# A fused state-space and channel-mixing kernel: its outer products in 64x32 tiles, more of them sharing a visit with other small-tile work

## The chip, the cores and the metric

The kernel runs on one core of one Trainium2 chip. The time is the device time of one execution in microseconds; several executions give a median. A profile is one execution taken by the hardware profiler. TensorE, which is PE in the rows, does the matrix products, and its weight loads are listed apart as PEld; VectorE is DVE, ScalarE is ACT, GpSimd is POOL and SyncE is SP. The last two mostly issue DMAs here.

## What is computed

The input x is 2048 tokens of 576 channels. After a layer norm it goes two ways: through a long convolution along the tokens, whose kernel K comes from 128 complex exponentials for each channel, and through a two-layer MLP for each token. The ways meet in a product.

```python
xn = layernorm(x)                                   # 2048 x 576
dt = exp(log_dt); A = -exp(log_A_real) + 1j * A_imag
C  = (C_real + 1j * C_imag) * dt[:, None]           # 576 x 128
P  = exp((A * dt[:, None])[:, :, None] * arange(2048))
K  = 2.0 * einsum("dn,dnl->dl", C, P).real
s  = irfft(rfft(xn, 4096) * rfft(K, 4096), 4096)[:2048] + xn * D_skip
h  = gelu(layernorm(xn) @ w1 + b1)                  # 4608 hidden
g  = silu(h @ w2 + b2)
out = x + s * g
```

All of it is in fp32. The MLP's matrices are split into a high and a low part in fp32r, and three products of parts stand for one.

## The kernel before

TensorE's work is of two kinds. The first is the MLP. The 4608 hidden columns come in 12 groups of three pieces of 128, the tokens in two halves of two blocks of 512, which makes 48 slots. A slot has layer 1 (`layer1`, its matmuls at L617, 128x512) for three pieces and then layer 2 (`layer2`, L680, 128x288) in eight steps. Between them `hidden` puts each piece through the GELU on ScalarE, a rounded copy on ScalarE (L656) and the low part on VectorE (L659).

The second kind is the convolution, in small tiles of the TensorE array, run on visits between steps of the MLP. The channels come in six chunks of 96 (`chunk`). Each chunk has

- stage 1 of the tokens (`x1`, matmuls at L1099 in tiles of 64 rows by 128 columns) and of the convolution kernel (`k1`, L1130, 32x128), both fed by a high and a low part made in `in_parts` (L1075 and L1079) and followed by transposes on VectorE (L1107, L1138);
- stage 2 (`s2`, L1160, 64x32, four times a chunk), followed by a copy on ScalarE (L1169) and complex products and sums on VectorE (L1175, L1181, L1182);
- the inverse (`inverse`, L1202, 32x64, two times a chunk) and the last stage (`i1`, L1228, 128x64), whose results go to memory.

The convolution's kernel is itself made on the chip in 36 batches of 16 channels. For each batch `load_par` (L896) loads parameters by a DMA that POOL issues, `tables` makes phases, sines and magnitudes on VectorE and ScalarE and weighs them (`weigh`, L950 to L956), and `kgen` forms the outer products (L995): for each channel, a product over the 128 exponentials, on the 128 rows of the array, of a table U of 32 columns and a table v of 64, real and imaginary part accumulated. Four channels stand side by side in the four column tiles of 32, so that a batch has 32 matmuls of fp32 in 128x32 tiles. The tables U and v lie in tiles of their own beside w, which holds the sines.

The order of all instructions is written out when the program is built. `Order` keeps a clock for each engine and a list of lines of steps, each with an engine, a reckoned duration, marks that it needs and a mark that it sets. After each step of the MLP, `pe_turns` decides whether small-tile work is put there. Outer products go alone, at the earliest `ALONE` after they could if the next batch's tables are not yet made or their due time isn't reached; or they ride: `ride` hands them to the stage that is put there (`GUEST`, `lead`), which then records them inside its own visit, in PSUM columns 384 to 511 of the host's bank. The inverse takes no riders. The clock then adds KG for the rider. At a slot's edge `pair` (L600) does the remaining 64 rows of layer 1 for two pieces side by side, in 64x128 tiles, in place of two full matmuls.

The durations that the planner reckons with are these:

```python
X1, S2, INV, I1, KG = 1.5, 1.75, 2.15, 3.05, 1.03
ALONE, DUE = 12.0, (160.0, 950.0)
```

In the first 50 us the rows of the input are loaded. `rest_of_norms` issues the loads of the last eight rows of tokens, and the step that issues them is reckoned to take 6 us until they land; behind it stand the statistics of those rows on VectorE (L407).

Of the kernel before, what the change touches and what calls it, by code (L numbers as in the profile page):

```python
# [18 lines left out]
P = 128  # L19
# [20 lines left out]
def dve(n):  # L40
    return 0.075 + 0.00104 * n
# [169 lines left out]
def mixer_kernel(ctx, tc, u, log_a_real, a_imag, c_real, c_imag, log_dt, d_skip, w1, b1, w2, b2,  # L211
# [38 lines left out]
    idp = sb.tile([P, P], F32, name="idp")  # L250
# [112 lines left out]

    def table_memory():

        t = [sb.tile([P, 2, SB, NV], F32, name="w", bufs=2) for _ in range(2)]
        t = [x.rearrange("p k c t -> p (k c t)") for x in t + [sb.tile([P, 2, SB, 64], F32, name="v")]]
        return [t[k // 3][:, k % 3 * D:(k % 3 + 1) * D] for k in range(8)]
# [418 lines left out]
    def params():  # L787
# [8 lines left out]
        dt = sb.tile([P, 2, SB, 32], F32, name="U").rearrange("p a b c -> p (a b c)")[:, :D]  # L796
# [94 lines left out]
    def load_par(b):  # L891
        if b == NB:
            return
        PAR[b] = sb.tile([P, SB, NPAR], F32, name="par", bufs=2)

        nc.gpsimd.dma_start(PAR[b].rearrange("p (g i) k -> p g (i k)", g=4), dram(  # L896
            par_s, (b // 3 * 48 + b % 3 * 4) * NPAR, [[D * NPAR, P], [12 * NPAR, 4], [1, 4 * NPAR]]))
# [7 lines left out]
    def tables(b):  # L905
# [5 lines left out]
        def phase(k):  # L911
            if k == 0:
                T["w"] = sb.tile([P, 2, SB, NV], F32, name="w", bufs=2)
# [28 lines left out]
        def weigh(k, part):  # L942

            if k == 0 and part == 0:
                T["v"] = sb.tile([P, 2, SB, 64], F32, name="v")
                T["U"] = sb.tile([P, 2, SB, 32], F32, name="U")
                TAB[b] = (T["U"], T["v"])
            w, v, m = T["w"], T["v"], T["m"]
            if part == 0:
                nc.vector.tensor_mul(T["U"][:, k], w[:, k, :, 33:], m[:, :, 64:])  # L950
            elif part == 1:
                nc.vector.tensor_mul(v[:, k, :, :32], w[:, k, :, 32:0:-1], m[:, :, :32])
            elif k == 0:
                nc.vector.tensor_mul(v[:, k, :, 32:], w[:, k, :, :32], m[:, :, 32:64])
            else:
                nc.vector.scalar_tensor_tensor(v[:, k, :, 32:], w[:, k, :, :32], -1.0, m[:, :, 32:64],  # L956
# [6 lines left out]
                 step("DVE", dve(SB * NV), f(phase, 0), need=[("wu", b - 2, 1)] if b > 1 else []),  # L963
# [6 lines left out]
                + [step("DVE", dve(n), f(weigh, k, part), need=[("sin", b, k)] + ([("kg", b - 1)] if b else []),  # L970
                        mark=("wu", b, k) if part == 2 else None) for k in range(2) for part in range(3)])
# [763 lines left out]
```

## Time and profile before

| | |
|---|---|
| median of 3 runs | 1099.31 us (1099.19 to 1099.48) |
| the profiled execution, as timed | 1101.59 us |
| its span from first to last instruction | 1099.8 us |
| granted clock of TensorE | 0.999 |
| HBM read and written | 102.17 MB and 36.63 MB |

A row of a group reads: source line, engine, operation, tile written, arrow, tiles read, for matmuls the array tile as rows*columns, shape and count; then busy time in us and the mean ns of one; then the idle time of the engine just before them and what ended it. A row of the timeline reads: start in us, from first start to last end in us, engine, line, operation and count. Matmuls overlap, so the time that a block takes is seen from its first start to the first start of what follows. "mxa" and "mxb" are the MLP's PSUM banks, "cv" those of the convolution.

### The profile page before, as it was taken

What the parts mean: (1) busy time and instruction counts of PE and PEld (TensorE: products, weight loads), DVE (VectorE), ACT (ScalarE), POOL (GpSimd) and SP (SyncE); (2) the same over time, 40 slices, a digit from 0 to 9 for tenths busy, and PEclk for the clock granted to TensorE, in tenths of its full rate; (3) what the DMA queues carried; (4) which work ended last, traced back from release to release, by engine and by line L of the source; (5) the groups of instructions that cost most, each with busy time, mean ns of one, the idle gap of its engine ahead of it and who ended that gap; (6) DMA issues with size and microseconds to landing.
All of it is one profiled execution on the core that took longest, in us unless ns stands there. A gap on an engine that the chain in (4) does not pass through costs nothing.

```text
span 1099.8 us, 27208 instructions
## 1 busy us (share of the span) xinstructions
PE 1089.1 (99%) x11445; PEld 953.2 (87%) x11445; DVE 918.8 (84%) x1514; ACT 698.0 (63%) x1044; POOL 184.0 (17%) x255
## 2 busy tenths in 40 slices
PE   8999999999999999999999999999999999999997
PEld 7889989889888888888898888888888888888897
DVE  7698678979998899999999998898998986766356
ACT  6485699867667675676865857566775754324233
POOL 4557211161110100001100000000100012110220
PEclk9999999999999999999999999999999999999999
DMA  8836656735434252355623315242333426453453
GB/s 222 242 131 169 219 173 197 215 71 130 152 115 152 53 112 57 100 128 149 154 51 95 96 56 126 39 143 59 94 89 78 145 66 178 117 178 107 128 148 94
DMA packets 139651, 138.23 MB, mean 126 GB/s; under 512 B 88952, under 2 KB 105016, under 8 KB 138952
## 3 DMA queue, kind: packets, MB, share of 16 engines
q1 hardware_dynamic: 124664, 85.49, 29.6%
q0 software_dynamic: 14384, 50.27, 14.8%
q8 instruction: 89, 1.46, 0.6%
q10 hardware_dynamic: 480, 0.74, 0.3%
q14 instruction: 34, 0.28, 0.1%
HBM read 102.17 MB, written 36.63 MB: 126 GB/s over the span
## 4 chain that ended last, share of the span: by engine, by line
PE 95%; DMA 2%; SPq 2%; DVE 1%; issue 0%; ACTq 0%; ACT 0%; DVEq 0%
PE mxb L680 21%; PE mxa L680 21%; PE mxa L617 20%; PE mxb L617 20%; PE cv L995 3%; PE cv L1160 3%; PE cv L1202 2%; PE cv L1228 2%; PE cv L1130 1%; PE cv L1099 1%; SPq L808 1%; DMA w<-in_A_u_dram 1%; DMA acc<-in_A_u_dram 0%; DVE st L407 0%; DMA h<-in_B_b_dram 0%
## 5 line engine op out<-in xcount | busy, mean ns | idle before, releaser
L659 DVE TENSOR_TENSOR hl<-h,hh 128x512 fp32r<-128x512 f32 x144 | 98.8, 689 | 89.0 <-ACT hh L656 88.3
L680 PE MATMUL mxb<-w2h,hl 128*128 128x288 f32 x576 | 170.2, 295 | 1.8 <-DVE hl L659 1.8
L680 PE MATMUL mxb<-w2h,hh 128*128 128x288 f32 x576 | 171.6, 298 | 0.0
L680 PE MATMUL mxa<-w2h,hh 128*128 128x288 f32 x573 | 170.8, 298 | 0.0
L680 PE MATMUL mxb<-w2l,hh 128*128 128x288 f32 x576 | 169.5, 294 | 0.0
L680 PE MATMUL mxa<-w2h,hl 128*128 128x288 f32 x573 | 169.2, 295 | 0.0
L680 PE MATMUL mxa<-w2l,hh 128*128 128x288 f32 x573 | 168.6, 294 | 0.0
L653 ACT ACTIVATE h<-mxa,b1t 128x512 f32<-128x512 f32 x73 | 50.2, 689 | 110.9 <-PE mxa L617 109.9
L680 PEld LDWEIGHTS mxa<-w2h,hh 128*128 128x128 f32 x573 | 107.6, 188 | 6.6 <-issue 3.5
L680 PEld LDWEIGHTS mxb<-w2h,hh 128*128 128x128 f32 x576 | 108.1, 188 | 5.7 <-issue 1.8
L680 PEld LDWEIGHTS mxb<-w2h,hl 128*128 128x128 f32 x576 | 108.1, 188 | 2.3 <-DVE hl L659 2.3
L680 PEld LDWEIGHTS mxb<-w2l,hh 128*128 128x128 f32 x576 | 108.1, 188 | 0.6
L680 PEld LDWEIGHTS mxa<-w2l,hh 128*128 128x128 f32 x573 | 107.6, 188 | 0.7
L680 PEld LDWEIGHTS mxa<-w2h,hl 128*128 128x128 f32 x573 | 107.5, 188 | 0.1
L896 POOL DMA_DIRECT2D par<-par_s x36 | 27.8, 773 | 462.9 <-DVE mg L939 458.4
L656 ACT ACTIVATE hh<-h 128x512 fp32r<-128x512 f32 x144 | 90.6, 630 | 3.6
L653 ACT ACTIVATE h<-mxb,b1t 128x512 f32<-128x512 f32 x71 | 48.9, 689 | 68.8 <-PE mxb L617 66.4
L690 DVE TENSOR_TENSOR acc<-mxa,acc 128x576 f32<-128x576 f32 x87 | 65.5, 752 | 31.2 <-PE mxa L680 30.9
L617 PE MATMUL mxa<-XH,w1h 128*128 128x512 f32 x284 | 79.1, 400 | 0.0
L690 DVE TENSOR_TENSOR acc<-mxb,acc 128x576 f32<-128x576 f32 x88 | 66.1, 752 | 15.2 <-PE mxb L680 14.8
L617 PE MATMUL mxb<-XH,w1h 128*128 128x512 f32 x280 | 77.7, 399 | 0.0
L617 PE MATMUL mxa<-XL,w1h 128*128 128x512 f32 x284 | 76.1, 390 | 0.0
(269 smaller groups left out, 2483.8 us busy)
## 6 DMA issues: line engine op xcount, KB each, us to landing
raw<-in_B_w_dram SPq DMA_DIRECT2D x72, 288.0 KB, 3.4
raw<-in_B_w_dram SPq DMA_DIRECT2D x96, 192.0 KB, 3.8
par_s<-A POOLq DMA_DIRECT2D x4, 2160.0 KB, 8.2
par<-par_s POOLq DMA_DIRECT2D x36, 240.0 KB, 3.4
f2t<-f2q SPq DMA_DIRECT2D x24, 256.0 KB, 3.4
g2t<-g2p SPq DMA_DIRECT2D x24, 256.0 KB, 4.1
bias<-XR SPq DMA_DIRECT2D x42, 128.0 KB, 3.7
raw<-in_B_w_dram SPq DMA_DIRECT2D x48, 96.0 KB, 3.9
```

Of the source, the lines that this page charges most:

```text
L617: nc.tensor.matmul(q, a, b, start=j == 0 and i not in BEGUN, stop=j == len(ops) - 1, skip_group_check=True)
L653: nc.scalar.activation(t, q, AF.Gelu_apprx_tanh, bias=b1t[:, k:k + 1], scale=1.0)
L656: LAST[0] = nc.scalar.activation(hh[:, i], t, AF.Copy)
L659: nc.vector.tensor_sub(hl[:, i], t, hh[:, i].bitcast(F32))
L680: nc.tensor.matmul(q[:, dh, :288], a[:, i, c], b[:, i, d], start=i == 0 and k == 0 and not alone, stop=i == G - 1 and k == 2)
L690: nc.vector.tensor_add(o, q[:, dh:dh + n, :288], b)
L808: nc.sync.dma_start(r[32 * g:32 * g + 32].rearrange("c (b n) -> c b n", n=32), dram(src[k], 32 * g, [[N, 32], [32 * N, D // 32], [1, 32]]))
L896: nc.gpsimd.dma_start(PAR[b].rearrange("p (g i) k -> p g (i k)", g=4), dram(par_s, (b // 3 * 48 + b % 3 * 4) * NPAR, [[D * NPAR, P], [12 * ...
L995: nc.tensor.matmul(q[32 * g:32 * g + 32, i // 2, i % 2 * 64:i % 2 * 64 + 64], U[:, ri, 4 * g + i, :], v[:, ri, 4 * g + i, :], start=ri == ...
L1160: nc.tensor.matmul(Q[i][32 * q:32 * q + 32, f, 2 * ri:2 * ri + 2], m[r, 4 * i + q, 32 * ri:32 * ri + 32], A2[r, 4 * p + 2 * i + q // 2, :, ...
L1202: nc.tensor.matmul(QI[q // 2][64 * f:64 * f + 64, q % 2, i], MAT["g2t", p + i // 2][r, i % 2, f, ri], YS[p + i // 2][0][r, i % 2, ri, f], ...
L1228: nc.tensor.matmul(Q[h][64 * y:64 * y + 64, t], g1t.rearrange("p a e -> p (a e)"), A2[:, k:k + 2, 1].rearrange("p i d r -> p i r d"), star ...
```

## The change

**Outer products.** `load_par` now loads a batch so that the upper 64 partitions hold other channels than the lower 64, and the 128 exponentials of a channel lie in two places of the same 64 partitions; four DMAs do it in place of one. `kgen` has 64 matmuls in 64x32 tiles: for each channel four accumulate, of two halves and two parts. U and v are now views of one tile with w, which `weigh` fills in place in four instructions instead of six.

**Rides.** A batch's outer products need one mark of the weighing (`wu`), the wait for the next batch's tables is for `wu` and not for the sines, and `ALONE` is 20 instead of 12. In stage 1 of the tokens the rider is recorded behind the host's matmuls instead of ahead of them. A ride with stage 2 is reckoned 0.14 us shorter than KG.

**Around them.** Stage 1's input is first put in order by one more copy on ScalarE, so that the high and the low part read contiguous memory. Transposes behind stage 1 are half as many and twice as long. Stage 2's results lie in another order in PSUM, its copy on ScalarE also writes a negated part, and products and sums are one instruction each. The last tokens' loads are reckoned 7 us instead of 6.

```diff
@@ -247,7 +247,7 @@
-    idp = sb.tile([P, P], F32, name="idp")
+    idp = sb.tile([P, 4, P], F32, name="f2t")[:, 0]
...
@@ -361,11 +361,13 @@
+    def table_tile():
+        return sb.tile([P, 2, SB, 32 + NV], F32, name="w", bufs=2)
+
     def table_memory():
-        t = [sb.tile([P, 2, SB, NV], F32, name="w", bufs=2) for _ in range(2)]
-        t = [x.rearrange("p k c t -> p (k c t)") for x in t + [sb.tile([P, 2, SB, 64], F32, name="v")]]
-        return [t[k // 3][:, k % 3 * D:(k % 3 + 1) * D] for k in range(8)]
+        t = [table_tile().rearrange("p k c t -> p (k c t)") for _ in range(2)]
+        return [t[k // 4][:, k % 4 * D:(k % 4 + 1) * D] for k in range(8)]
...
@@ -893,8 +895,12 @@
-        nc.gpsimd.dma_start(PAR[b].rearrange("p (g i) k -> p g (i k)", g=4), dram(
-            par_s, (b // 3 * 48 + b % 3 * 4) * NPAR, [[D * NPAR, P], [12 * NPAR, 4], [1, 4 * NPAR]]))
+        for h in range(2):
+            for e in range(2):
+                nc.gpsimd.dma_start(
+                    PAR[b][64 * h:64 * h + 64, 8 * e:8 * e + 8].rearrange("p (g i) k -> p g (i k)", g=4), dram(
+                        par_s, (64 * e * D + b // 3 * 48 + b % 3 * 4 + 2 * h) * NPAR,
+                        [[D * NPAR, 64], [12 * NPAR, 4], [1, 2 * NPAR]]))
...
@@ -939,36 +946,34 @@
-        def weigh(k, part):
-
-            if k == 0 and part == 0:
-                T["v"] = sb.tile([P, 2, SB, 64], F32, name="v")
-                T["U"] = sb.tile([P, 2, SB, 32], F32, name="U")
-                TAB[b] = (T["U"], T["v"])
+        def weigh(part):
+
+            if part == 0:
+                TAB[b] = (T["w"][:, :, :, 33:], T["v"][:, :, :, :64])
             w, v, m = T["w"], T["v"], T["m"]
             if part == 0:
-                nc.vector.tensor_mul(T["U"][:, k], w[:, k, :, 33:], m[:, :, 64:])
+                nc.vector.tensor_mul(v[:, :, :, :32], w[:, :, :, 32:0:-1], bc(m[:, :, :32], 1, 2))
             elif part == 1:
-                nc.vector.tensor_mul(v[:, k, :, :32], w[:, k, :, 32:0:-1], m[:, :, :32])
-            elif k == 0:
-                nc.vector.tensor_mul(v[:, k, :, 32:], w[:, k, :, :32], m[:, :, 32:64])
+                nc.vector.tensor_mul(w[:, :, :, 33:], w[:, :, :, 33:], bc(m[:, :, 64:], 1, 2))
+            elif part == 2:
+                nc.vector.tensor_mul(w[:, 0, :, :32], w[:, 0, :, :32], m[:, :, 32:64])
             else:
-                nc.vector.scalar_tensor_tensor(v[:, k, :, 32:], w[:, k, :, :32], -1.0, m[:, :, 32:64],
+                nc.vector.scalar_tensor_tensor(w[:, 1, :, :32], w[:, 1, :, :32], -1.0, m[:, :, 32:64],
...
-                 step("DVE", dve(SB * NV), f(phase, 0), need=[("wu", b - 2, 1)] if b > 1 else []),
+                 step("DVE", dve(SB * NV), f(phase, 0), need=[("kg", b - 2)] if b > 1 else []),
...
-                + [step("DVE", dve(n), f(weigh, k, part), need=[("sin", b, k)] + ([("kg", b - 1)] if b else []),
-                        mark=("wu", b, k) if part == 2 else None) for k in range(2) for part in range(3)])
+                + [step("DVE", dve((2, 2, 1, 1)[part] * n), f(weigh, part), need=[("sin", b, 1)],
+                        mark=("wu", b) if part == 3 else None) for part in range(4)])
...
@@ -989,18 +994,21 @@
             Q.append(q)
-            for i in range(SB // 4):
-                for ri in range(2):
+            for i in range(2):
+                for k in range(4):
+                    ri, e = divmod(k, 2)
                     for g in range(4):
-                        nc.tensor.matmul(q[32 * g:32 * g + 32, i // 2, i % 2 * 64:i % 2 * 64 + 64], U[:, ri, 4 * g + i, :],
-                                         v[:, ri, 4 * g + i, :], start=ri == 0, stop=ri == 1, skip_group_check=True)
+                        for h in range(2):
+                            f, t = slice(64 * h, 64 * h + 64), 8 * e + 2 * g + i
+                            nc.tensor.matmul(q[32 * g:32 * g + 32, h, 64 * i:64 * i + 64], U[f, ri, t, :], v[f, ri, t, :],
+                                             start=k == 0, stop=k == 3, skip_group_check=True)
...
-        return [step("PE", KG + 0.2, mm, need=need + [("wu", b, 1)], cv=1, mark=("kg", b)),
+        return [step("PE", KG + 0.2, mm, need=need + [("wu", b)], cv=1, mark=("kg", b)),
...
@@ -1013,7 +1021,7 @@
         GUEST.append(st["fn"])
-        host["dur"] += KG
+        host["dur"] += KG - 0.14 * (host["mark"][0] == "s2")
...
@@ -1068,19 +1076,28 @@
+            T = {}
+
+            def turn():
+                T["x"] = sb.tile([P, 24, m], F32, name="xt")
+                nc.scalar.activation(T["x"], get(), AF.Copy)
+
+            def source():
+                return get() if which == "k" else T["x"].rearrange("p c b -> p (c b)")
+
             def high():
-                a = sb.tile([P, 2, 4 * CH], F32R, name="pr").rearrange("p t c -> p (t c)")
-                b = sb.tile([P, 2, 4 * CH], F32R, name="ys", bufs=2).rearrange("p t c -> p (t c)")
-                PARTS2[which, i] = [t.rearrange("p (c b) -> p c b", b=m) for t in (a, b)]
-                nc.scalar.activation(PARTS2[which, i][0], get(), AF.Copy)
+                T["a"] = sb.tile([P, 2, 4 * CH], F32R, name="pr").rearrange("p t c -> p (t c)")
+                T["b"] = sb.tile([P, 2, 4 * CH], F32R, name="ys", bufs=2).rearrange("p t c -> p (t c)")
+                PARTS2[which, i] = [T[k].rearrange("p (c b) -> p c b", b=m) for k in "ab"]
+                nc.scalar.activation(T["a"], source(), AF.Copy)
             def low():
-                a, b = PARTS2[which, i]
-                nc.vector.tensor_sub(b, get(), a.bitcast(F32))
-
-            n = 768 if which == "k" else 2000
-            four.append(step("ACT", act(n), high, need=need))
-            four.append(step("DVE", dve(n), low, mark=(which + "p", c, i)))
+                nc.vector.tensor_sub(T["b"], source(), T["a"].bitcast(F32))
+
+            if which == "x":
+                four.append(step("ACT", act(2000), turn, need=need))
+            four.append(step("ACT", act(768), high, need=need if which == "k" else ()))
+            four.append(step("DVE", dve(768), low, mark=(which + "p", c, i)))
...
@@ -1091,21 +1108,20 @@
                     Q[24 * v] = q[:, :, :384].rearrange("p e (d b) -> p e d b", b=32)
-                lead(q)
...
+                lead(q)
...
-                for e in range(2):
-                    c0 = 48 * i + d0 + 12 * e
-                    add("DVE", 0.65, lambda d0=d0, e=e, c0=c0: nc.vector.transpose(
-                        A2[:, :, 0, c0:c0 + 12].rearrange("p k d r -> p d k r"), Q[d0][:, e]), cv=-e)
+                c0 = 48 * i + d0
+                add("DVE", 0.9, lambda d0=d0, c0=c0: nc.vector.transpose(
+                    A2[:, :, 0, c0:c0 + 24].rearrange("p k d r -> p d k r"), Q[d0]), cv=-1)
...
@@ -1134,11 +1150,9 @@
             add("PE", X1, mm, cv=2, mark=("k1", c, i), need=[("kp", c, i)] + ([("i1", c - 1)] if c and i == 0 else []))
-            for g in range(4):
-                add("DVE", 0.65, lambda g=g: nc.vector.transpose(
-                    A2[:, :, 1, 48 * i + 12 * g:48 * i + 12 * g + 12].rearrange("p k d r -> p d k r"),
-                    Q[g // 2 * 2][:, g % 2]),
-                    cv=-(g % 2))
+            for g in (0, 2):
+                add("DVE", 0.9, lambda g=g: nc.vector.transpose(
+                    A2[:, :, 1, 48 * i + 12 * g:48 * i + 12 * g + 24].rearrange("p k d r -> p d k r"), Q[g]), cv=-1)
...
@@ -1157,7 +1171,7 @@
                                 r = slice(64 * f, 64 * f + 64)
-                                nc.tensor.matmul(Q[i][32 * q:32 * q + 32, f, 2 * ri:2 * ri + 2],
+                                nc.tensor.matmul(Q[i][32 * q:32 * q + 32, f, ri::2],
...
@@ -1165,25 +1179,26 @@
             def copy(i):
-                KK[i] = sb.tile([P, 2, 2, CH], F32, name="kk")
-                nc.scalar.activation(KK[i], Q[i][:, :, 1::2], AF.Copy)
+                KK[i] = sb.tile([P, 2, 3, CH], F32, name="kk")
+                nc.scalar.activation(KK[i][:, :, :2], Q[i][:, :, :1:-1], AF.Copy)
+                nc.scalar.activation(KK[i][:, :, 2], Q[i][:, :, 3], AF.Copy, scale=-1.0)
...
-                PR[i] = sb.tile([P, 2, 4 * CH], F32, name="pr").rearrange("p t (a b d) -> p t a b d", a=2, b=2)
-                for t in range(2):
-                    nc.vector.tensor_mul(PR[i][:, t], bc(Q[i][:, t, 0::2], 2, 2), bc(KK[i][:, t], 1, 2))
+                PR[i] = sb.tile([P, 2, 4 * CH], F32, name="pr").rearrange("p t (a c) -> p t a c", a=2)
+                x, k = Q[i].rearrange("p t k d -> p t (k d)")[:, :, :2 * CH], KK[i].rearrange("p t k d -> p t (k d)")
+                k = bass.AP(tensor=k.tensor, offset=k.offset + CH, ap=[list(k.ap[0]), list(k.ap[1]), [-CH, 2], [1, 2 * CH]])
+                nc.vector.tensor_mul(PR[i], bc(x, 2, 2), k)
...
-                nc.vector.tensor_sub(y[:, i, 0], x[:, :, 0, 0], x[:, :, 1, 1])
-                nc.vector.tensor_add(y[:, i, 1], x[:, :, 0, 1], x[:, :, 1, 0])
+                nc.vector.tensor_add(y[:, i].rearrange("p a t d -> p t a d"), x[:, :, :, :CH], x[:, :, :, CH:])
             for i in range(2):
-                two.append(step("ACT", act(4 * CH), lambda i=i: copy(i), need=[("s2", c, p)]))
-                two.append(step("DVE", 0.95, lambda i=i: prod(i), cv=-1))
-                two.append(step("DVE", 0.63, lambda i=i: sums(i), mark=("sum", c, p) if i else None))
+                two.append(step("ACT", act(4 * CH) + act(2 * CH), lambda i=i: copy(i), need=[("s2", c, p)]))
+                two.append(step("DVE", dve(8 * CH), lambda i=i: prod(i), cv=-1))
+                two.append(step("DVE", dve(4 * CH), lambda i=i: sums(i), mark=("sum", c, p) if i else None))
...
@@ -1456,7 +1471,7 @@
             x_load(b)
-    nl["steps"].append(step(None, 6.0, rest_of_norms))
+    nl["steps"].append(step(None, 7.0, rest_of_norms))
...
@@ -1518,7 +1533,7 @@
     EDGE = 0.2, 0.6
-    ALONE, DUE = 12.0, (160.0, 950.0)
+    ALONE, DUE = 20.0, (160.0, 950.0)
...
@@ -1536,7 +1551,7 @@
                     b = kl["steps"][0]["mark"][1]
-                    wait = ("sin", b + 1, 1) not in od.marks or od.t["PE"] < DUE[0] + b * (DUE[1] - DUE[0]) / NB
+                    wait = ("wu", b + 1) not in od.marks or od.t["PE"] < DUE[0] + b * (DUE[1] - DUE[0]) / NB
...
```

More of the change, by code (lines that the diff above doesn't have):

```diff
@@ L795, in params @@
         flat = lambda t: t.rearrange("p a b -> p (a b)")
[L796 removed]
+        dt = ys_tile().rearrange("p i a b c -> p (i a b c)")[:, :D]
         PRM = [flat(sb.tile([P, 12, 64], F32, name="kt", bufs=2)) for _ in range(2)]
@@ L912, in phase @@
             if k == 0:
-                T["w"] = sb.tile([P, 2, SB, NV], F32, name="w", bufs=2)
+                T["v"] = table_tile()
+                T["w"] = T["v"][:, :, :, 32:]
                 nc.vector.tensor_mul(T["w"][:, 1], bc(PAR[b][:, :, 0], 2, NV), bc(tv, 1, SB))
```

2 lines of the change are left out of this document (1 added, 1 removed).

## The prediction

> **What bounds the kernel now.** First the page: its shares of busy time, then its chain of work that ended last.
>
> ```profile
> span 1099.8 us, 27208 instructions
> PE 1089.1 (99%) x11445; PEld 953.2 (87%) x11445; DVE 918.8 (84%) x1514; ACT 698.0 (63%) x1044; POOL 184.0 (17%) x255
> PE 95%; DMA 2%; SPq 2%; DVE 1%; issue 0%; ACTq 0%; ACT 0%; DVEq 0%
> ```
>
> TensorE is busy 99% of the span and carries 95% of the chain. Next, what TensorE waited for in the whole execution:
>
> ```profile
> PE mxb L680 <- DVE hl L659: 1.8, 2, 1.2
> PE mxa L1290 <- POOL XL L1283: 1.3, 1, 1.3
> PE cv L500 <- DVE row L440: 1.1, 1, 1.1
> PE mxa L632 <- ACT XH L504: 0.4, 1, 0.4
> ```
>
> That is 4.6 us, all before 50 us. So the end is set by the sum of TensorE's own work. Work saved on VectorE or added on ScalarE moves nothing while it only fills idle time; a microsecond of TensorE moves the end by one. The third view groups TensorE's instructions by shape; these are the groups that the change bears on:
>
> ```profile
> L995 PE MATMUL cv<-v,U 128*32 128x64 f32 x2304 | 39.6, 221 | 0.0
> L1160 PE MATMUL cv<-A,f2t 64*32 64x192 f32 x1536 | 38.6, 332 | 0.0
> L1202 PE MATMUL cv<-ys,g2t 32*64 32x96 f32 x1536 | 21.9, 253 | 0.0
> ```
>
> Each fp32 matmul of the source shows as two MATMUL records and two weight loads: the outer products (L995) are 1152 in the source and 2304 here, 36 blocks of 64. Stage 2 (L1160) is 24 blocks of 64, the inverse (L1202) 12 blocks of 128. These durations overlap, so the price of a block is read from the timeline as the distance from its first start to the next block's first start:
>
> ```profile
> 361.57 0.29 PE L680 MATMUL mxb<-w2l,hh 128*128 128x288 f32 x1
> 361.70 0.29 PE L680 MATMUL mxb<-w2h,hl 128*128 128x288 f32 x1
> 361.92 1.10 PE L995 MATMUL cv<-v,U 128*32 128x64 f32 x64
> 362.95 0.40 PE L680 MATMUL mxa<-w2h,hh 128*128 128x288 f32 x1
> 363.19 0.29 PE L680 MATMUL mxa<-w2l,hh 128*128 128x288 f32 x1
> ...
> 296.54 1.58 PE L1160 MATMUL cv<-A,f2t 64*32 64x192 f32 x64
> 298.05 0.40 PE L680 MATMUL mxa<-w2h,hh 128*128 128x288 f32 x1
> ...
> 440.12 1.10 PE L995 MATMUL cv<-v,U 128*32 128x64 f32 x64
> 441.15 1.62 PE L1160 MATMUL cv<-A,f2t 64*32 64x192 f32 x64
> 442.70 1.21 PE L617 MATMUL mxb<-XH,w1h 128*128 128x512 f32 x4
> ...
> 325.66 1.83 PE L1202 MATMUL cv<-ys,g2t 32*64 32x96 f32 x128
> 327.42 1.20 PE L617 MATMUL mxb<-XH,w1h 128*128 128x512 f32 x4
> ```
>
> Outer products alone take 361.92 to 362.95, 1.03 us. Going in costs 0.22 instead of the usual 0.13 from start to start, and the first MLP matmul behind takes 0.24 instead of 0.13: 0.20 us for each visit that the small tiles pay between MLP matmuls. Stage 2 takes 1.51 alone and 1.55 behind outer products, the inverse 1.76.
>
> **The outer products in 64x32 tiles.** The same multiplications now come as 64 source matmuls a block over eight tiles (two halves of the rows, four of the columns) instead of 32 over four: 128 records and 128 weight loads instead of 64 and 64. No row shows this. By columns nothing changes: 64 records over four tiles are 16 rounds of 64 columns, 1024 in 1.03 us, 1.0 ns a column; 128 over eight are again 16 rounds of 64. Lower end: 1.03 us. Stage 2, also over eight tiles, keeps that rate: 8 rounds of 192 columns, 1536, in 1.51. But it has only 64 records. The inverse has 128 over eight tiles, 16 rounds of 96, the same 1536 columns, and takes 1.76: 0.22 to 0.25 more than its columns ask. So many short records have a price that columns do not explain. Upper end: a new block is as long as the inverse, 1.76. How the inverse loses it, in two narrow stretches of the timeline:
>
> ```profile
> 325.66 0.43 PEld L1202 LDWEIGHTS cv<-ys,g2t 32*64 32x64 f32 x33 [0.35 <-issue]
> 325.66 0.59 PE L1202 MATMUL cv<-ys,g2t 32*64 32x96 f32 x32
> ```
>
> The stretches end at 326.04. The first 32 matmuls have started after 0.35 us (0.59 less the 0.24 of the last one), 11 ns each, and only one weight load stands beyond them. The other 96 need the remaining 1.41 us, 14.7 ns each. I read this as a limit on how many instructions TensorE holds at once: after 32 pairs the next must wait until an early matmul has ended, and that wait goes by a matmul's whole duration, not by its columns. The old outer products escape it: 64 pairs at a slower beat, two batches.
>
> [...]
>
> For the new block: the first 32 at the rate of columns, 16 pairs a round-time of 112 ns, 0.22 us; the other 96 like the inverse's, 1.41 us, times the ratio of the durations in the rows above, 221/253: 1.23. Together **1.45 us**, 0.42 more than now, 36 blocks: **+15.1 us**. Other readings lie on both sides: the inverse's excess as a fixed 0.23 gives 1.26, its late beat kept whole 0.22 + 1.41 = 1.63.
>
> **Rides.** In the two programs' instruction order, runs of small-tile work between MLP matmuls are 84 before and 76 after; 18 of 36 outer products stand alone before and 10 after. Eight visits less at 0.20: **-1.6 us**. Twelve outer products share a visit with stage 2 in both. After the change both are in 64x32 tiles. What a shared shape saves is seen where the paired remainder (L600) and stage 1 (L1099), both 64x128, stand side by side:
>
> ```profile
> 254.31 0.50 PE L600 MATMUL mxb<-XR,w1s 64*128 64x512 f32 x1
> 254.65 0.51 PE L1099 MATMUL cv<-pr,f2t 64*128 64x384 f32 x4
> 255.81 0.96 PE L617 MATMUL mxb<-XH,w1h 128*128 128x512 f32 x3
> ...
> 240.36 0.62 PE L1099 MATMUL cv<-pr,f2t 64*128 64x384 f32 x4
> 241.63 1.20 PE L617 MATMUL mxa<-XH,w1h 128*128 128x512 f32 x4
> ...
> 439.69 0.50 PE L600 MATMUL mxb<-XR,w1s 64*128 64x512 f32 x1
> ```
>
> Side by side 0.34 and 1.16; alone stage 1 takes 1.27, and ahead of outer products L600 takes 0.43 (439.69 to 440.12). That saves 0.20; the lower end is the 0.04 by which stage 2 is longer behind outer products. I take 0.15, twelve times: **-1.8 us**. Moving the rider behind stage 1's matmuls puts stage 1 next to L600 in two visits, as in two before: nothing. Two more L600 pairs replace four full matmuls: under 0.1.
>
> **The last tokens' landing.** VectorE takes its work in order, and L407 waits there for the loads:
>
> ```profile
> 43.78 0.82 DVE L407 BATCH_NORM_STATS2 st<-w 128x6 f32<-128x288 f32 x2 [3.77 <-DMA w<-in_A_u_dram]
> 44.94 0.46 DVE L407 BATCH_NORM_STATS2 st<-w 128x6 f32<-128x288 f32 x1
> 45.32 0.67 DVE L659 TENSOR_TENSOR hl<-h,hh 128x512 fp32r<-128x512 f32 x1
> ```
>
> TensorE's 1.8 us on L659 is this. In the changed order only the statistics at 44.94 move behind L659; the two at 43.78, which wait for the load, stay ahead. So 0.4 comes back: **-0.4 us** (0 to -1.8).
>
> **VectorE, ScalarE, POOL.** The merged table products, transposes, products and sums save starts of instructions, and the contiguous low part saves more; stage 1's input is copied once more on ScalarE:
>
> ```profile
> L1079 DVE TENSOR_TENSOR ys<-xc,pr 128x768 fp32r<-128x768 f32 x12 | 24.7, 2056 | 1.8 <-ACT pr L1075 1.6
> L1079 DVE TENSOR_TENSOR ys<-kt,pr 128x768 fp32r<-128x768 f32 x12 | 11.1, 927 | 0.0
> L1075 ACT ACTIVATE pr<-kt 128x768 fp32r<-128x768 f32 x12 | 10.1, 838 | 4.3 <-PE cv L1099 3.8 <-ACT w2h L570 0.3 <-PE cv L1130 0.3
> L896 POOL DMA_DIRECT2D par<-par_s x36 | 27.8, 773 | 462.9 <-DVE mg L939 458.4
> ```
>
> Strided against contiguous: 2056 - 927 = 1.1 us, 12 times, 14 us off VectorE; 12 x 0.84 = 10 us onto ScalarE, and 48 negating copies of at most 0.3, 14 more. The cover is TensorE's 99%: no wait on either engine ends late after 50 us, so I take 0; without the cover ScalarE's 24 us would be the ceiling. L896 becomes four issues: 144 x 0.77 = 111 us on POOL instead of 28, 3.1 us a batch, behind which POOL's stores queue. POOL idled 463 us before these issues, and the load is asked for a batch ahead of its use (950 - 160 over 36 by the planner, 22 us); hidden.
>
> **Sum** against the profiled span: +15.1 - 1.6 - 1.8 - 0.4 = +11.3, 1111.1. The runs' median of 1099.31 lies 0.5 under the span of 1099.8, so **1110.6 us**.
>
> **Rivals.** First, TensorE keeps the rate of columns: a block stays at 1.03. For it: stage 2 over eight tiles at 1.51, no dearer than its columns. Against it: the inverse with the same count of records. Then -3.8 us, **1095.5**, faster; it decides up to a block of 1.07, where -3.8 + 36 x 0.04 leaves the 0.2% of gain. Second, the excess is small and the two sides meet: a block of 1.07 to 1.20 gives 1097 to 1101.5, at 1.14 **1099.5**, no change beyond the 0.2% (2.2 us) that a measurement of this kernel can tell. The inverse's fixed excess with half of it hidden (1.03 + 0.11) speaks for it. Third, the parameter loads come late through POOL's four issues: the table work then blocks VectorE with L659 behind it. At 2.3 us (3 x 0.77) for each of the three or four batches that start before 160 us, on top of the forecast, **1118**; POOL's 17% speaks against.
>
> **How the numbers follow.** Forecast, blocks of 1.26 to 1.63: 53%; by itself 36 x 0.23 - 3.8 = +4.5 to 36 x 0.60 - 3.8 = +17.8, 1104 to 1117. First rival 32%, second 12%, third 3%. The range reaches down to the first rival and leaves out the top of the forecast: 1094.8 to 1114.5. Faster 0.33, same 0.12, slower 0.55.
>
> **What would show it.** In the changed profile the outer products' group has 4608 records in tiles of 64x32. Right: about 1.45 us from the first of 128 records to the next block, the start beat slower after the first 32. Wrong: 1.03 with an even beat. Shared visits with stage 2 should be 0.15 shorter than their parts; TensorE's waits should stay near 4 us and before 50 us. A wait of TensorE on VectorE or ScalarE after 60 us would show that a cover is gone, and a wait of L939 on the parameter load the third rival.

## The result and the profile after

| | before | after |
|---|---|---|
| median of 5 runs | 1099.48 us | 1137.40 us (1136.98 to 1139.60) |
| span of the profiled execution | 1099.8 us | 1135.3 us |
| ratio, 95% interval | | 1.0346 (1.0330 to 1.0363) |

The change costs 38 us: the direction of the forecast, three times its size, and outside its range. The profiled execution of before was timed at 1101.59 us, 2.3 above the median, so the spans differ by 35.5 us where the medians differ by 37.9. The changed kernel's page, shares of busy time, chain by engine, and the queue that brings instructions; behind it that queue's row from the page of before:

```profile
span 1135.3 us, 31836 instructions
PE 1109.2 (98%) x13749; PEld 969.5 (85%) x13749; DVE 892.4 (79%) x1298; ACT 731.5 (64%) x1112; POOL 244.2 (22%) x363
PE 81%; DVE 5%; DMA 5%; ACT 4%; issue 3%; POOL 1%; SPq 0%; DVEq 0%; ACTq 0%; POOLq 0%
q8 instruction: 107, 1.75, 0.7%
```

```profile
q8 instruction: 89, 1.46, 0.6%
```

TensorE still looks full, 98%. But its part of the chain has fallen from 95% to 81%, and 3% stand at "issue", time in which nothing that the profile records held it. What TensorE waited for, in the changed kernel (us in total, times, longest):

```profile
PE cv L1174 <- issue: 8.8, 6, 2.4
PE mxa L619 <- ACT h L655: 2.4, 1, 2.4
PE mxb L682 <- DVE acc L692: 1.8, 1, 1.8
...
PE mxb L682 <- issue: 1.1, 2, 0.7
```

Two things are new: six waits in stage 2 (L1174, before L1160) with no releaser, and waits on ScalarE and VectorE, which the forecast had excluded after 50 us. The groups and the timeline of the changed kernel give the price of a new block:

```profile
L1003 PE MATMUL cv<-w 64*32 64x64 f32 x4608 | 53.7, 225 | 0.0
L1174 PE MATMUL cv<-A,f2t 64*32 64x192 f32 x1536 | 42.9, 338 | 8.8 <-issue 8.8
```

```profile
156.59 1.49 PE L1003 MATMUL cv<-w 64*32 64x64 f32 x128
158.00 0.74 PE L619 MATMUL mxb<-XH,w1h 128*128 128x512 f32 x2
```

1.41 us from first start to first start, where it was 1.03. Summed by line over both traces, as distances from start to start (a stop counts with what it takes beyond the ordinary beat, and the slower starts right behind it), the span's 35.5 us divide so:

| after less before | us |
|---|---|
| outer products, 36 blocks: 37.1 to 49.7 | +12.6 |
| stage 2, 24 blocks: 36.9 to 49.9, of it 9.9 in six stops | +13.0 |
| stops in the MLP: 2.7 to 14.0, of it about 8 between 97 and 171 us | +11.3 |
| the MLP without its stops (fewer visits, four matmuls fewer) | -2.1 |
| two more L602 pairs, the rest | +0.7 |

The forecast had the first and the fourth row; stage 2 it had with the other sign, the third row not at all. Nearly all of stage 2's 13 us lie in the six blocks that stop: they take 2.79 to 5.38 us from first start to the next block's first start, 22.0 together, while the other six behind outer products take 1.54 to 1.59, 9.4 together. One of those that run through, with the outer products ahead of it:

```profile
774.13 1.48 PE L1003 MATMUL cv<-w 64*32 64x64 f32 x128
775.42 1.65 PE L1174 MATMUL cv<-A,f2t 64*32 64x192 f32 x64
777.00 1.19 PE L619 MATMUL mxa<-XH,w1h 128*128 128x512 f32 x4
```

### The profile page after: what moved, and what is told of

Read it like the earlier page. It is cut to its first block, busy times and chain, and to the rows that moved or that the text cites. A ratio compares the mean times of both kernels' runs of the same rounds, so it can differ in the third digit from the quotient of the medians.

```text
span 1135.3 us, 31836 instructions
## 1 busy us (share of the span) xinstructions
PE 1109.2 (98%) x13749; PEld 969.5 (85%) x13749; DVE 892.4 (79%) x1298; ACT 731.5 (64%) x1112; POOL 244.2 (22%) x363
## 3 DMA queue, kind: packets, MB, share of 16 engines
q0 software_dynamic: 16112, 50.27, 15.1%
q8 instruction: 107, 1.75, 0.7%
## 4 chain that ended last, share of the span: by engine, by line
PE 81%; DVE 5%; DMA 5%; ACT 4%; issue 3%; POOL 1%; SPq 0%; DVEq 0%; ACTq 0%; POOLq 0%
PE mxb L682 17%; PE mxa L682 17%; PE mxa L619 17%; PE mxb L619 16%; PE cv L1003 4%; PE cv L1174 3%; DMA par_s<-A 2%; PE cv L1217 2%; PE cv L1146 1%; PE cv L1243 1%; PE cv L1115 1%; DMA kk<-in_f_dram 1%; DMA f2p<-in_f_dram 1%; DVE w2l L569 1%; DMA row<-y_s 1%
## 5 line engine op out<-in xcount | busy, mean ns | idle before, releaser
L900 POOL DMA_DIRECT2D par<-par_s x144 | 88.9, 633 | 350.8 <-DVE mg L946 268.7
L692 DVE TENSOR_TENSOR acc<-mxa,acc 128x576 f32<-128x576 f32 x87 | 65.5, 753 | 26.5 <-PE mxa L682 26.3
L692 DVE TENSOR_TENSOR acc<-mxb,acc 128x576 f32<-128x576 f32 x88 | 66.1, 752 | 22.7 <-PE mxb L682 22.4
```

The source lines that it names most:

```text
L692: nc.vector.tensor_add(o, q[:, dh:dh + n, :288], b)
L900: nc.gpsimd.dma_start(PAR[b][64 * h:64 * h + 64, 8 * e:8 * e + 8].rearrange("p (g i) k -> p g (i k)", g=4), dram(par_s, (64 * e * D + b // ...
```

## What the experiments showed

Three theories had to be told apart: the dearer blocks (foreseen), stops because TensorE's instructions do not arrive in time, and a changed early order that comes from one number of the planner. The ratios are to the kernel before.

**The outer products taken back out.** `load_par` and the matmuls of `kgen` are those of before; all else is as changed.

```diff
-            for i in range(2):
-                for k in range(4):
...
+            for i in range(SB // 4):
+                for ri in range(2):
                     for g in range(4):
+                        nc.tensor.matmul(q[32 * g:32 * g + 32, i // 2, i % 2 * 64:i % 2 * 64 + 64], U[:, ri, 4 * g + i, :],
```

> The changed kernel with the outer products and the parameter load put back (32 matmuls in 128x32 tiles, one DMA); tables, rides, stages and book-keeping stay as changed. Theory: three things make the 38 us: the longer blocks (36 x 0.35 to 0.39, 13 us), waits of TensorE for its own instructions around them (12 to 15 us), and an early order that makes it wait for VectorE and ScalarE between 100 and 170 us (6 to 8 us). Then this version loses the first two: 1108 to 1112 us, blocks of 1.03, no stop inside stage 2, and the early waits still there. Rival: the new steps on ScalarE and VectorE (copies, merged products) are what TensorE waits for: then it stays above 1125 us.

Measured 1112.54, 1.0117 (1.0097 to 1.0137), half a microsecond above the range of the theory. The blocks are back at 1.03 and of the stops in stage 2 one of 0.2 us is left; what stays is early:

```profile
PE mxa L619 <- ACT h L655: 5.7, 1, 5.7
```

So the new outer products cost 25 us in place of the 13 of their blocks, and the rest of the change costs 13 without them.

**The outer products alone**, put into the kernel before (the same edit the other way round).

> The kernel before with nothing but the new outer products and the four parameter loads they need. Theory: +13 us from blocks of about 1.41 instead of 1.03, and on top stops of 1 to 2.6 us inside some of the twelve stage 2 blocks that come right behind outer products, 5 to 12 us: 1117 to 1125 us, no new waits before 170 us. Rival one: no such stops, they come from the changed stage 2: 1112 us. Rival two: the blocks are longer only because of the tables' new place in memory (a row pitch of 97): 1099 to 1102 us.

Measured 1122.89, 1.0216 (1.0194 to 1.0238): 23 us again from this part. The blocks sum to 49.9 us (49.7 in the changed kernel) though U and v lie in tiles of their own as before, so the second rival, the tables' place in memory, is refuted. The stops are there (waits and timeline of this kernel), and its rides are those of before:

```profile
PE cv L1167 <- issue: 6.3, 6, 1.3
```

```profile
714.97 1.20 PE L617 MATMUL mxa<-XH,w1h 128*128 128x512 f32 x4 [0.74 <-issue]
```

The second fence shows one that is not in stage 2: it meets layer 1, behind a visit of outer products with stage 1 of the convolution's kernel. Stage 2 is not the cause, only the usual place.

**What makes a block long: records or columns.** Two kernels halve the one and the other. In the first, half of the accumulation is left out; in the second, half of v's columns, and a second copy on ScalarE fills the place.

```diff
-                for k in range(4):
+                for k in (0, 2):
...
-                                             start=k == 0, stop=k == 3, skip_group_check=True)
+                                             start=k == 0, stop=k == 2, skip_group_check=True)
```

> The changed kernel with only the first half of each accumulation in the outer products (the exponentials of the second half are left out): 64 records over eight tiles, still in stage 2's shape. Theory: TensorE holds some 32 pairs at a time, so two batches instead of four: blocks of 0.75 to 0.85 us instead of 1.41, and no stop inside stage 2, since 128 + 128 instructions are no more than before: 1098 to 1106 us with the early waits still there. Rival: the stops come from the shape that stage 2 shares with what stands ahead of it: they stay, 10 us, 1110 to 1116 us.

```diff
-                            nc.tensor.matmul(q[32 * g:32 * g + 32, h, 64 * i:64 * i + 64], U[f, ri, t, :], v[f, ri, t, :],
+                            nc.tensor.matmul(q[32 * g:32 * g + 32, h, 32 * i:32 * i + 32], U[f, ri, t, :], v[f, ri, t, :32],
```

> The changed kernel with outer products of 32 moving columns instead of 64 (half of the table v is left out, the other half is copied twice by two smaller copies): the records stay 128 a block, the columns are halved. Theory: the block goes by records and by a matmul's whole duration, which falls only by some 27 ns of 225: 1.30 to 1.38 us. Rival: it goes by columns (16 rounds of 32): 0.6 to 0.8 us. Stops inside stage 2 stay under the theory, they are about the count of instructions; time 1133 to 1138 us.

Timeline of the one with half the records, then of the one with half the columns:

```profile
156.06 0.86 PE L1003 MATMUL cv<-w 64*32 64x64 f32 x64
156.84 1.19 PE L619 MATMUL mxb<-XH,w1h 128*128 128x512 f32 x4
```

```profile
190.96 1.29 PE L1003 MATMUL cv<-w 64*32 64x32 f32 x128
192.18 0.40 PE L682 MATMUL mxa<-w2h,hh 128*128 128x288 f32 x1
```

Half the records: 0.78 us. Half the columns: 1.22, less than the 1.30 to 1.38 of the theory and far from the rival's 0.6 to 0.8. From 1.41 the first takes 0.63, the second 0.19. Half the records are half the columns too, so 0.44 of the 0.63 are left for the records alone: their number sets most of the price, as the forecast had it. That it is a limit on what TensorE holds is a reading that fits both, not shown by itself. The stops go the same way: with half the records the only wait left in stage 2 is one of 0.2 us on a DMA, with half the columns six stops remain.

```profile
L1174 PE MATMUL cv<-A,f2t 64*32 64x192 f32 x1536 | 39.3, 333 | 0.2 <-DMA f2t<-f2q 0.2
```

```profile
PE cv L1175 <- issue: 10.1, 6, 2.1
```

By time the first took 1106.35 us, the second 1136.16, one run each: halving the columns saved next to nothing of the 38 us. The first shows too how much is not outer products: its blocks are 10 us cheaper than before's, and it is 7 us slower all the same.

**Why TensorE stops: the supply of instructions.** The row of q8 above gives 1.75 MB in 107 packets, 16.4 KB each, and TensorE has 27498 records, 257 for each packet. One stop in the changed kernel, by its timeline, and the queues in the window 449 to 453:

```profile
449.67 0.59 PE L1003 MATMUL cv<-w 64*32 64x64 f32 x35
450.06 0.91 PE L1174 MATMUL cv<-A,f2t 64*32 64x192 f32 x29
452.25 1.21 PE L1174 MATMUL cv<-A,f2t 64*32 64x192 f32 x35 [1.28 <-issue]
```

```profile
q8 instruction: 1, 0.02, 1.5%
```

Stage 2 halts after 29 of its 64 matmuls and goes on at 452.25; the one packet of q8 there ran from 449.80 to 450.75 in the trace. A block of outer products with stage 2 behind it is 256 + 128 loads and matmuls in about 3 us; the MLP, with a load and a matmul every 0.13 or 0.23 us, needs 8 to 15 us for 128 instructions. The six stops in stage 2 come after 9640, 10662, 11173, 17558, 19088 and 23176 records; from one to the next are 1022, 511, 6385, 1530 and 4088, each within 15 of a multiple of 256. If pieces of 256 instructions are the cause, the stops must fall on their borders, and move over the work when something is put ahead. Two kernels put 64 and 128 short matmuls more into the warm-up, 128 and 256 instructions:

```diff
-    warm_up(16)
+    warm_up(8)
+    for _ in range(72):
+        nc.tensor.matmul(qb[:, 0, :64], zero[:, :P], zero[:, :64], start=True, stop=True)
```

> The changed kernel with 64 short matmuls more in the warm-up ahead of everything: 128 more instructions of TensorE (64 loads, 64 matmuls) before all others, the same order behind them. Theory (TensorE's instructions come in pieces of 256, and a stop falls on the border of two pieces): counted in TensorE's records of loads and matmuls, the six stops in stage 2 of the changed kernel come after 9640, 10662, 11173, 17558, 19088 and 23176 records, with rests of 168 falling to 136 by 256. Shifted by 128, the borders fall elsewhere in the work: all six of those stage 2 blocks (near 450, 484, 497, 743, 790 and 926 us) run through, and 2 to 6 stops come at others whose last 256 instructions took under 2 us: near 346, 358, 594, 614, 643 or 910 us, again with a rest of 136 to 170. Rival (something in those six blocks themselves stops them: their place in the order, their bank, what they read): the same six stop, with rests of about 10 to 40.

The second has 4 and 140 there.

> The changed kernel with 128 short matmuls more in the warm-up: 256 more instructions of TensorE before all others, the same order behind them. Theory: the borders of pieces fall on the same work again; if every border can stop TensorE, the same six stage 2 blocks stop, with the same rests. If only every other border can (borders that stopped lie mostly 512 or a multiple apart), most of the six run through and others, near 775 us among them, may stop. Rival (the blocks themselves): the same six, as also in the run with 128 more.

The waits of TensorE in the kernel shifted by 128, and its timeline; then the waits of the one shifted by 256:

```profile
PE cv L1174 <- issue: 6.9, 4, 2.7
...
PE cv L1146 <- issue: 2.3, 1, 2.3
```

```profile
357.72 0.88 PE L1174 MATMUL cv<-A,f2t 64*32 64x192 f32 x21
361.31 0.56 PE L1174 MATMUL cv<-A,f2t 64*32 64x192 f32 x11 [2.70 <-issue]
...
470.18 1.65 PE L1174 MATMUL cv<-A,f2t 64*32 64x192 f32 x64
```

```profile
PE cv L1174 <- issue: 9.9, 6, 2.8
```

The two kernels took 1150.83 and 1165.98 us, one run each; most of what they take more than the changed kernel is the longer warm-up itself, behind which the first matmul of layer 1 starts at 24.1 and 39.3 us instead of 13.0. Shifted by 128, all six old places run through; the block that stood at 450 is the one at 470.18, 64 matmuls without a break. Five of the six places named ahead stop instead (at 361, 377, 612, 634 and 926 us of this run, whose work lies 15 to 20 us later); the sixth, the one foreseen at 643, loses only 0.3 us. Shifted by 256, the same six stop as in the changed kernel. How many records had started at a stop is read from windows that end there; of the changed kernel, of the shift by 128 and by 256, with the counts of PE and PEld in brackets:

```profile
0.00:452.24 452.24, 442.36 (x4820) 391.00 (x4820) 358.75 (x552) 315.07 (x507) 146.93 (x203) 1.00 0.52 147
```

```profile
0.00:376.88 376.88, 365.39 (x3670) 326.40 (x3670) 283.17 (x451) 253.30 (x427) 134.84 (x184) 0.97 0.55 158
```

```profile
0.00:478.62 478.62, 469.43 (x4948) 419.82 (x4948) 357.78 (x552) 315.23 (x507) 147.39 (x203) 1.00 0.49 139
```

9640, 7340 and 9896 records leave 168, 172 and 168 by 256. All stops without a releaser in small tiles have such a rest, in these kernels and in the one with the outer products alone, from 179 falling to 136 as the run goes on. Three of the MLP's stops in the changed kernel (616, 644 and 913 us, 2.1 us together) have it too.

The packets of q8 tell which borders stop. In the changed kernel each of the eight stops without a releaser ends 1.4 to 1.6 us after the end of the q8 packet before it (452.25 against 450.75 above; 743.27 against 741.88 at the longest), and in the two shifted kernels and the one with the outer products alone it is 1.2 to 1.6. Packets and borders go one to one: border 37 of the run, at 9640 records, stops for the 37th packet, and so for every stop. A border near 775 us was passed without a stop, though its last 256 instructions took 1.3 us: its packet had ended at 773.03, and TensorE came to the border at 775.4, 2.4 us later. With the rests of the other borders estimated from those of the stops, nine of the changed kernel's borders were reached less than 1.4 us after the end of their packet, and these are the six stops in stage 2 and the three in the MLP; the next one came 1.6 us after and did not stop. So the cause is shown: in the changed kernel TensorE waited at a border when it came there less than about 1.4 us after the packet with the next piece had landed. What sets the time of a packet stays open: at the eight stops it starts between 251 records ahead of the border and, at the longest, only when TensorE stands there. That a shift by one piece brought the same six back shows that it is not a fixed every other one.

**Rides with stage 2 refused**, so that outer products and stage 2 stand apart.

```diff
-        if not kl["steps"] or kl["steps"][0]["eng"] != "PE" or host["mark"][0] == "inv":
+        if not kl["steps"] or kl["steps"][0]["eng"] != "PE" or host["mark"][0] in ("inv", "s2"):
```

> The changed kernel in which outer products do not ride with stage 2. Theory: the stops inside stage 2 (six of 0.9 to 2.6 us beyond the ordinary beat, 10 us) come from 256 + 128 instructions used up in 3 us; apart, they are gone, and some 3 us of slower stage 2 behind outer products go as well, while eight more visits cost 1.6 us and the shared shape's 1.3 us are lost: 1126 to 1130 us. Rival: the stops belong to stage 2's changed order of columns in PSUM and stay: 1139 to 1141 us.

Measured 1155.33, 1.0509 (1.0487 to 1.0531), a miss by time. Of the stops one of 0.5 us is left (first fence, waits; its rest by 256 is 139), and TensorE's last matmul starts 7 us earlier than in the changed kernel. But the order became another one: the last stage of the convolution ran at 1104 (timeline), 30 us later than in the changed kernel, and the chain ends in its stores and loads.

```profile
PE cv L1174 <- issue: 0.5, 1, 0.5
```

```profile
1104.11 2.92 PE L1243 MATMUL cv<-A,g1t 128*64 128x384 f32 x16
```

```profile
1108.22 4.51 DMA s_s<-ys
...
1140.80 4.60 DMA A<-s_s
```

After TensorE's last matmul 32 us of such work remain, 6 in the other kernels. It tells that the stops go when outer products and stage 2 stand apart, and that an edit of the planner cannot be priced by the part that it is meant for.

**One number of the planner: the last tokens' landing.** In the changed kernel it is put back from 7 to 6 us; in the kernel before, it is put from 6 to 7 with nothing else touched.

```diff
-    nl["steps"].append(step(None, 7.0, rest_of_norms))
+    nl["steps"].append(step(None, 6.0, rest_of_norms))
```

> The changed kernel with the last tokens' landing reckoned 6 us again. Theory: that number moved the second half of the norms and all that hangs on it on POOL some 20 us later; with 6 the waits of TensorE between 100 and 170 us go (8 us) and the two at 45 and 48 us come back (1.8 us): 1130 to 1133 us. Rival: the early order is another because of the changed tables and tiles, and the waits stay: 1136 to 1139 us.

Measured 1127.48, 1.0255 (1.0237 to 1.0274): 10 us less than the changed kernel and less than either expectation. The waits between 97 and 171 us are gone; those at 45 and 48 us, which were expected back, did not come; the stops in stage 2 stay (10.3 us, eight times, in its waits).

> The kernel before with nothing but the last tokens' landing reckoned 7 us. Theory: it takes back up to 1.8 us at 45 and 48 us and moves the second half of the norms on POOL later; if that alone makes the waits at 147 to 161 us, 1102 to 1108 us. Rival: in the kernel before the early order has room for it: 1097 to 1099 us, give or take the four visits more that its order has (0.8 us).

Measured 1111.81, 1.0116 (1.0099 to 1.0133): the number alone costs 12 us, more than the theory had. What it does is read in the timelines, first the kernel before, then the changed one:

```profile
81.28 2.79 POOL L450 TENSOR_SCALAR w<-w,mv,rs 128x576 f32<-128x576 f32 x1 [7.76 <-ACT h L653]
...
94.67 0.57 POOL L271 DMA_DIRECT2D turns_s<-in_f_dram  x1
...
138.42 0.55 POOL L883 DMA_DIRECT2D par_s<-A  x1 [11.53 <-ACT w2h L570]
...
148.99 5.31 ACT L874 ACTIVATE A<-A 128x144 f32<-128x144 f32 x18
...
155.61 0.69 ACT L653 ACTIVATE h<-mxa,b1t 128x512 f32<-128x512 f32 x1
```

```profile
93.34 2.28 POOL L452 TENSOR_SCALAR w<-w,mv,rs 128x576 f32<-128x576 f32 x1 [21.08 <-issue]
...
123.13 0.56 POOL L271 DMA_DIRECT2D turns_s<-in_f_dram  x1
...
144.29 0.58 POOL L885 DMA_DIRECT2D par_s<-A  x1 [2.48 <-DMA f2p<-in_f_dram]
...
156.63 5.26 ACT L876 ACTIVATE A<-A 128x144 f32<-128x144 f32 x18 [8.59 <-DMA par_s<-A]
...
163.21 0.69 ACT L655 ACTIVATE h<-mxa,b1t 128x512 f32<-128x512 f32 x1
```

In the changed order the norms of the last rows come 12 us later on POOL, and with them the constants (28 us later) and a store of parameters (6 us later). The kernel before with nothing but the 7 us has the same: its norms start at 93.72, its constants at 121.83, the store at 142.46. ScalarE then stood 8.59 us for that store's landing, and the rest of the table work (L876) and the GELU came only behind it: the GELU starts at 163.21 and TensorE waited for it, 2.4 us. On VectorE the same happened with the constants, and TensorE's 1.8 us on L692 are this:

```profile
147.83 0.23 DVE L294 TENSOR_TENSOR kk<-kk 128x64 f32<-128x64 f32 x1 [2.98 <-DMA kk<-turns_s]
148.99 0.75 DVE L692 TENSOR_TENSOR acc<-mxb,acc 128x576 f32<-128x576 f32 x1
```

In the kernel before with 7 us the wait is longer, and TensorE is slow behind it; its waits, and two windows (the first bare number after the busy times is the granted clock):

```profile
PE mxa L617 <- ACT h L653: 6.0, 1, 6.0
```

```profile
158.00:165.00 7.00, 1.00 (x5) 0.53 (x3) 3.67 (x4) 6.97 (x22) 0.00 (x0) 0.85 0.09 30
165.00:170.00 5.00, 5.00 (x13) 3.90 (x14) 2.63 (x3) 4.48 (x8) 0.00 (x0) 0.52 0.01 3
```

In the 5 us behind the wait only 13 matmuls ran, at a granted clock of 0.52; the kernel before has 40 there at 1.00. The changed kernel with the old outer products shows it again (5.7 us of waiting, then 12 matmuls in 5 us at 0.50); the changed kernel waits 2.4 us and stays at 1.00.

**What is left of the change.** Old outer products and 6 us together; then also the full reckoning for rides with stage 2 (`host["dur"] += KG`); then, from the first again, `ALONE` 12 instead of 20.

> The changed kernel with the old outer products and load, and the landing reckoned 6 us again. Theory: with the blocks, the supply stops and the early waits gone, what is left is the rides (12 visits less than before the change, 2.4 us), against small waits on VectorE and ScalarE of 1 to 4 us that the change's planning brings: 1097 to 1102 us. Rival: the changed stages and tables cost TensorE several microseconds by themselves: 1105 us or more.

> As the version with the old outer products and the landing of 6, with a ride with stage 2 reckoned at KG in full. Theory: the 6 us of small waits of TensorE on VectorE and ScalarE in that version come in part from a plan that reckons each such ride 0.14 us short of what the old tiles take, so that later work is planned for a TensorE that is further on than it is; then 1098 to 1100.5 us. Rival: they come from the new steps on ScalarE and the tables, whatever the reckoning: 1101 to 1103 us.

> As the version with the old outer products and the landing of 6, with ALONE at 12 us as before the change. Theory: rides are worth 0.20 us for each visit saved and nothing else, so two visits more cost 0.4 us and the time is 1101.5 to 1103 us. Rival: holding the outer products back for 20 us is what brings the small waits: 1098 to 1100.5 us.

| kernel | us | ratio |
|---|---|---|
| old products, landing 6 | 1102.03 | 1.0022 (1.0012 to 1.0031) |
| the same, full reckoning | 1102.13 | 1.0025 (1.0017 to 1.0034) |
| the same as the first, `ALONE` 12 | 1100.90 | 1.0010 (1.0002 to 1.0019) |

The first lies at the top of its theory's range, the second in its rival's, the third between the two. The reckoning of rides does nothing that can be measured; a longer `ALONE` costs about 1 us at most, the two intervals overlap. None of the three beats the kernel before. The first has no wait between 97 and 171 us and 72 visits in place of 84. Summed as above, its visits take some 2 us less, and short waits in the MLP, spread over the run, some 4 us more; two of them:

```profile
PE mxa L682 <- DVE acc L692: 1.0, 1, 1.0
PE mxb L682 <- DVE hl L661: 0.9, 2, 0.5
```

The parts add up: outer products alone +23.3 against the kernel before on the same chip, the landing alone +12.3, the rest +2.5, together 38.1 where the change costs 37.9. That they meet so closely is in part luck: taken out of the changed kernel, the outer products give 24.9 and the landing 9.9, and the two early waits are not the same length.

## Why the prediction was right or wrong

- **A block of outer products, 1.45 us, +15.1:** right. 1.41 where it stands alone, 1.28 ahead of stage 2; +12.6 in all. The first 32 matmuls start within 0.27 us (0.22 in the sum), the rest at a slower beat, as the working had it. By halving, more of it goes by the records than by the columns (0.44 to 0.19). The first two rivals, the rate of columns and the small excess, are refuted.
- **Shared shape with stage 2, 0.15 each:** right in size where nothing stops: 1.41 less 1.28 is 0.13, and stage 2 behind it is 0.02 longer than alone. But the sum took no account of what those visits bring close together, 384 loads and matmuls within 3 us. This term had the wrong sign: -1.8 forecast, some +11 with the stops.
- **Eight visits fewer, -1.6:** right as far as it can be read: the MLP without its stops is 2.1 us shorter, and 0.9 of that are four matmuls fewer at 0.23, which the two more pairs give back.
- **The missing term: the supply of instructions.** The block was priced by what TensorE does with an instruction, not by how it gets one. The page of before had a row on it, q8 with 89 packets for 22890 records, and from that the 107 could be reckoned, but not the waiting: before has no wait without a releaser. It is a term that the sum put at nothing without a reason. About 12 us counted as stops, six of 9.9 and three of 2.1; 12.6 in stage 2 alone, counted as what the six blocks take beyond the six that run through.
- **The last tokens' landing, -0.4:** with the supply of instructions, the step that failed by most. Even its local part is not shown: before's 1.8 us on L659 at 45 us are gone from the changed kernel, but also from the kernel with the outer products alone, which has before's early order and 6 us; the load had come there by 40.15 instead of 43.78. The step looked only at the instructions around the loads, but the number moves the planner's clock, and with it POOL's norms, the constants and the parameters, up to 28 us. +12 by itself, +10 taken out of the changed kernel.
- **VectorE, ScalarE, POOL at 0 because TensorE's 99% covers them:** wrong. What TensorE waited for in the old order did not carry over to the new one. ScalarE's 8.59 us behind par_s and VectorE's 2.98 behind kk passed through to TensorE; the text had named a wait after 60 us as the sign that a cover is gone, and that sign is there.
- **The third rival, parameter loads late through POOL's four issues:** refuted. The outer products alone have the four issues and no new early wait, the changed kernel with the one old load keeps its early wait, and a load lands in 2.4 us at 450 us.
- **The range:** its upper bound of 1114.5 was made from the block's price, and lies below the 1117 that the working itself gave as the top of the forecast. The landing was bounded at nothing, the supply of instructions had no term. That the time moved the way that was forecast is the block's doing; that it moved by 38 us is not in the working.

## What to carry to other kernels

Count the instructions that TensorE gets within a few microseconds, not only their durations: twice the records in small tiles cost here as much again in supply as in work, some 12 us each, and such bursts should not stand side by side. Where an order is made by a planner, a changed duration is a change of the whole order, so read both orders past the edited place, on POOL and ScalarE too, before a term is called local. Run the one-number edit alone.

## What the runs showed of the hardware that was not expected

- In the changed kernel TensorE stopped at the nine borders of 256 instructions that it reached less than about 1.4 us after the packet that brought the next piece, and not at one that it reached 1.6 us after. In the shifted kernels the waits were up to 2.8 us; they fell on other work when 128 instructions were put ahead, and returned when 256 were.
- Eight of these nine stops had no releaser in the profile, and TensorE's busy share stayed at 98%; the releaser "issue", in the chain (3%) and in the view of waits, told them.
- A wait of 6.0 us had 5 us behind it at a granted clock of 0.52, with 13 matmuls in place of 40; one of 5.7 us had 0.50 behind it, one of 2.4 us 1.00.
